# A fused attention and MoE kernel: moe_w_out loaded by column halves, and the second layer's first halves placed among units 5 and 6

## Chip, cores and metric

One Trainium2 chip, one core. The metric is the device time of the kernel in microseconds (us); a profile's own span is some 1.7 us shorter than the time of the same run.

## The reference, cut to what matters

A recurrence over 768 steps (4 batches, 8 heads, head size 48) gives 3072 rows of 384 numbers; two layers follow.

```python
for t in range(S):                      # S = 768
    cur = einsum('bhd,bhe->bhde', u * k[t], v[t])
    y[t] = einsum('bhd,bhde->bhe', r[t], state + cur)
    state = w * state + einsum('bhd,bhe->bhde', k[t], v[t])
x = y.transpose(0, 2, 1, 3).reshape(3072, 384)
h = x @ w_in                            # 384 x 2048
g = h * (1.0 / (1.0 + exp(-h)))
return g @ w_out                        # 2048 x 384
```

## The kernel before

Time is cut into 6 chunks of 128 steps; a **unit** is one chunk of one batch, so there are 24, numbered chunk * 4 + batch. A unit loads r, k and v (`load`), has its rows turned (`p1t`, `p1d`), its scores multiplied and masked (`p2`), its output `y` made (`p3y`, `p3e`), its state brought forward (`sums`, `state`), and its output turned for the two layers (`p4`).

The two layers are **fillers**: a queue of small pieces, taken by `fill(n)` wherever TensorE (PE) would else wait for the recurrence. A first-layer piece for two batches (a "half group": 3 matmuls of 256 columns and one ScalarE activation) has weight 0.5; a second-layer part has weight 1. Both kinds take their PSUM tile from the same three banks (tag `moe`).

```python
    def l1(sc, ft, b0=0, b1=B):                     # first layer
        hps = ps.tile([128, B * C], FP, name="hps", tag="moe", bufs=3)
        ...                                         # 3 matmuls, then ScalarE:
        nc.scalar.activation(out=gts[sc][:, ft, b0 * C:b1 * C], in_=hps, func=AF.Silu)

    def l2(sc, b, part):                            # second layer: 4 parts for each batch
        if part == 0:
            opss[b] = ps.tile([128, HD], FP, name="ops", tag="moe", bufs=3)
        ops = opss[b]
        for ft in range(4 * part, 4 * part + 4):
            nc.tensor.matmul(ops, gts[sc][:, ft, b * C:(b + 1) * C], wout[:, ft, :], ...)
        if part == 3:
            osb = wrk.tile([128, HD], FP, name="osb", bufs=4)
            nc.vector.tensor_copy(out=osb, in_=ops)
            nc.sync.dma_start(out=out[tt:tt + C, :], in_=osb)

    def fill(n):
        owed[0] = min(owed[0] + n, n + 1.0)
        while fillers and owed[0] > 0.01:
            w_, f = fillers.pop(0)
            owed[0] -= w_
            f()
    ...
    def wout_part(g):                               # rows 1024 g to 1024 g + 1023, cast to float16
        nc.gpsimd.dma_start(out=wout[:, 8 * g:8 * g + 8, :], in_=moe_w_out[...])
    ...
    # unit 5 is b_ = B + 1
    p2(b_, nxt=b_ + 1, late=True)                   # with unit 6's turn among unit 5's scores
    fill(1.5)
    p3y(b_)
    p3e(b_)
    p1d(b_ + 1)
    sums(2)
    state(2)
    fill(.5)
    p4(b_)
    fill(1)
    f = l2s(0)
    fillers.extend(l1s(1, 0, 2) + f[0:2] + f[4:6] + f[2:4] + f[6:])
    ...
    for i in range(B + 2, NU):                      # units 6 to 23
        ...
        if i == B + 2:
            half_state(3)                           # float32 state to float16, on ScalarE
        fill(1)
        if sc == 1:
            half_state(b)
        fill(1 if sc in (2, 3) else 2)
```

Of the kernel before, what the change touches and what calls it, by code (L numbers as in the profile page):

```python
# [8 lines left out]
FP = mybir.dt.float32  # L9
# [6 lines left out]
def kernel(  # L16
# [11 lines left out]
    nc = tc.nc  # L28

    B, H, S, D = r.shape  # L30
    C = 128
    NCH = S // C
    HD = H * D
# [4 lines left out]
    NFT = DFF // 128  # L38
# [7 lines left out]
    wrk = ctx.enter_context(tc.tile_pool(name="wrk", bufs=2))  # L46
    ps = ctx.enter_context(tc.tile_pool(name="ps", bufs=1, space=bass.MemoryType.PSUM))
# [11 lines left out]
    wout = big.tile([128, NFT, HD], F16)  # L59

    def unit(i):
        return divmod(i, B)
# [31 lines left out]
    for t in (rin, kin):  # L94
# [7 lines left out]
        out=maskM, in_=maskM, compare_op=ALU.is_ge, fill=0.0,  # L102
# [17 lines left out]
    def spin(n, t=None):  # L120

        if t is None:
            t = ps.tile([128, 512], FP, name="spin", tag="t", bufs=5)
        else:
            t = t.rearrange("s p t -> s (p t)")
        for _ in range(n):
            nc.tensor.matmul(t, junk[:, 0:128], junk, start=True, stop=True)  # L127
# [32 lines left out]
    n = 1  # L160
    while n < C:
        nc.vector.tensor_tensor(
            out=pi[:, :, 1 + n:1 + 2 * n], in0=pi[:, :, 1:1 + n],
# [6 lines left out]
    def lam(g):  # L170

        t = pif.rearrange("q (a n) -> q a n", a=2)[:, :, 0:NT]
        return t.rearrange("q a (p c) -> q a p c", c=C + 1)[:, :, :, 64 * g:64 * g + 64]
# [9 lines left out]
    def nat_ku(i):  # L183
        L = live.setdefault(i, {})
        L["ku"] = wrk.tile([128, H, D], FP, name="ku")
        nc.gpsimd.tensor_tensor(out=L["ku"], in0=kin[i % NIN][:, :, 0:D], in1=u_bc,  # L186
                                op=ALU.mult)

    def nat_rk(i):
        L = live[i]  # L190
        L["rku_f"] = wrk.tile([128, H, D], FP, name="rku_f")
        nc.gpsimd.tensor_tensor(out=L["rku_f"], in0=rin[i % NIN][:, :, 0:D], in1=L["ku"],  # L192
                                op=ALU.mult)

    def nat_kc(i):
        n = i % NIN
        nc.gpsimd.tensor_tensor(out=kc[i % NKC][:, :, 0:D], in0=kin[n][:, :, 0:D],  # L197
                                in1=lamC, op=ALU.mult)
# [37 lines left out]
    def p1t(i):  # L236

        n = i % NIN
        L = live.setdefault(i, {})
        xs = [ps.tile([128, 2, NP, 64], FP, name="xs", tag="t", bufs=5) for _ in range(2)]  # L240
        for a, src in enumerate((rin, kin)):
            flat = src[n].rearrange("p h d -> p (h d)")
            for p in range(NP):
                for g in range(2):
                    t = slice(64 * g, 64 * g + 64)
                    nc.tensor.transpose(xs[g][0:PR, a, p, :],  # L246
                                        flat[t, 128 * p:128 * p + PR], ident[t, t])
        rk = wrk.tile([PR, 2, NP, C], FP, name="rk")
        L["rT"] = rk[:, 0]
        L["kT"] = rk[:, 1]  # L250
        L["xs"] = xs, rk

    def p1d(i):
        L = live[i]
        xs, rk = L["xs"]
        for g in range(2):
            nc.vector.tensor_tensor(out=rk[:, :, :, 64 * g:64 * g + 64], in0=xs[g][0:PR],  # L257
                                    in1=lam(g), op=ALU.mult)
# [6 lines left out]
    def p2(i, spins=0, nxt=None, late=False):  # L265
        L = live[i]
        ae = ps.tile([128, NP, C], FP, name="ae", tag="t", bufs=5)
        ao = ps.tile([128, NP, C], FP, name="ao", tag="t", bufs=5)
        spin(spins, ae)
        for p in range(NP):  # L270
            nc.tensor.matmul(ae[:, p, :], L["kT"][0:D, p, :], L["rT"][0:D, p, :],  # L271
                             start=True, stop=True)
            nc.tensor.matmul(ao[:, p, :], L["kT"][64:PR, p, :], L["rT"][64:PR, p, :],  # L273
                             start=True, stop=True)
        if nxt is not None:
            p1t(nxt)
        L["am"] = []
        for a in (ae, ao):
            am = wrk.tile([128, NP, C], F16, name="am", bufs=4)
            nc.vector.tensor_tensor(out=am, in0=a,  # L280
                                    in1=maskM.unsqueeze(1).broadcast_to([128, NP, C]),
                                    op=ALU.mult)
            L["am"].append(am)
        if nxt is not None and not late:
            p1d(nxt)
# [15 lines left out]
    def p3e(i):  # L301
        L = live[i]
        L["y16"] = wrk.tile([128, H, D], F16, name="y16", bufs=3)
        nc.vector.tensor_tensor(out=L["y16"], in0=L["y"], in1=L["vu"], op=ALU.add)  # L304
# [49 lines left out]
    gts = {}  # L354

    def l1(sc, ft, b0=0, b1=B):
        if sc not in gts:
            gts[sc] = wrk.tile([128, NFT, B * C], F16, name="gT", bufs=2)
        hps = ps.tile([128, B * C], FP, name="hps", tag="moe", bufs=3)
        hps = hps[:, 0:(b1 - b0) * C]  # L360
        for q in range(NQ):
            nc.tensor.matmul(hps, win[:, q, ft * 128:(ft + 1) * 128],  # L362
                             xts[sc][:, q, b0:b1, :].rearrange("p b t -> p (b t)"),
                             start=(q == 0), stop=(q == NQ - 1))
        nc.scalar.activation(out=gts[sc][:, ft, b0 * C:b1 * C], in_=hps, func=AF.Silu)  # L365

    opss = {}

    def l2(sc, b, part):
        if part == 0:  # L370
            opss[b] = ps.tile([128, HD], FP, name="ops", tag="moe", bufs=3)
        ops = opss[b]
        for ft in range(4 * part, 4 * part + 4):
            nc.tensor.matmul(ops, gts[sc][:, ft, b * C:(b + 1) * C], wout[:, ft, :],  # L374
                             start=(ft == 0), stop=(ft == NFT - 1))
        if part == 3:
            osb = wrk.tile([128, HD], FP, name="osb", bufs=4)
            nc.vector.tensor_copy(out=osb, in_=ops)  # L378
            tt = b * S + sc * C
            nc.sync.dma_start(out=out[tt:tt + C, :], in_=osb)  # L380

    def l2_last(sc, b):

        tt = b * S + sc * C
        for n0, n1 in ((0, 256), (256, HD)):
            ops = ps.tile([128, HD], FP, name="ops", tag="moe", bufs=3)
            for ft in range(NFT):
                nc.tensor.matmul(ops[:, n0:n1], gts[sc][:, ft, b * C:(b + 1) * C],  # L388
                                 wout[:, ft, n0:n1],
                                 start=(ft == 0), stop=(ft == NFT - 1))  # L390
            osb = wrk.tile([128, HD], FP, name="osh")
            nc.vector.tensor_copy(out=osb[:, n0:n1], in_=ops[:, n0:n1])
            nc.sync.dma_start(out=out[tt:tt + C, n0:n1], in_=osb[:, n0:n1])

    def l1s(sc, b0=0, b1=B):
        return [((b1 - b0) / B, lambda ft=ft: l1(sc, ft, b0, b1)) for ft in range(NFT)]

    def l2s(sc, b0=0, b1=B):
        return [(1.0, lambda b=b, part=part: l2(sc, b, part))
                for b in range(b0, b1) for part in range(4)]  # L400

    fillers = []
    owed = [0.0]

# [6 lines that stand above are left out]
# [5 lines left out]
    def win_part(c0, c1):  # L416
        nc.gpsimd.dma_start(out=win[:, :, c0:c1],  # L417
                            in_=moe_w_in[:, c0:c1].rearrange("(q p) n -> p q n", p=128))

    def wout_part(g):  # L420
        nc.gpsimd.dma_start(
            out=wout[:, 8 * g:8 * g + 8, :],
            in_=moe_w_out[1024 * g:1024 * g + 1024, :].rearrange("(f p) n -> p f n", p=128))


    p1(0)
# [68 lines left out]
    a, b_ = B, B + 1  # L495
    nat_ku(a)
    nat_rk(a)
    nat_kc(3)
    fill(1)
    p4(3)  # L500
    fill(1000)
# [5 lines left out]
        nat_kc(i)  # L507


    fillers.extend(l1s(0, 2, 4))  # L510
    p1t(a)
    p1d(a)
    bonus_sum(a)
# [10 lines left out]
    p2(a, nxt=b_)  # L524
    nat_ku(b_)
    nat_rk(b_)
    fill(1)
    p3y(a)
    p3e(a)
    wout_part(0)  # L530
    sums(1)
    state(1)
    bonus_sum(b_)
    bonus_vu(b_)
    nat_kc(b_)
    wout_part(1)
    fill(1)
    sums(a)
    state(a)
# [4 lines left out]
    nat_v(b_)  # L544
    for i in range(4):
        load(NIN + i)
    p2(b_, nxt=b_ + 1, late=True)
    fill(1.5)
    p3y(b_)
    p3e(b_)  # L550
    p1d(b_ + 1)
    sums(2)
    state(2)
    fill(.5)
    p4(b_)
    fill(1)
    f = l2s(0)
    fillers.extend(l1s(1, 0, 2) + f[0:2] + f[4:6] + f[2:4] + f[6:])
    sums(b_)
    state(b_)  # L560
    fill(.5)
# [8 lines left out]
    for i in range(B + 2, NU):  # L570
        sc, b = unit(i)
# [27 lines left out]
        if b == B - 1:  # L599
            if sc == 1:  # L600
                f = l1s(1, 2, 4)
# [35 lines left out]
```

## Time and profile before

| | before |
|---|---|
| time, median | 197.33 us (3 runs; 197.08 to 197.41) |
| PE busy, share of the span | 97% |
| matmuls | 1916 |
| unit 5's scores start | 34.45 us |
| unit 6's scores start | 41.17 us |
| unit 13's scores start | 90.04 us |
| unit 23's scores start | 161.49 us, 34.5 us before the end |

The starts of the scores are read from PE's timeline (the first `ae` matmul of a unit). PE is full nearly everywhere, so a shift between two such marks is either idle time or filler put in or taken out.

### The profile page before, as it was taken

Reading aid. Unit: us, or ns where it says so; the run is one execution under the profiler, and the core shown is the slowest. Engines: PE = TensorE matmul, PEld = TensorE weight load, DVE = VectorE, ACT = ScalarE, POOL = GpSimd, SP = SyncE. Lnnn points to the kernel's source line nnn. Section 1 sums busy time; section 2 is a strip of 40 time slices with the busy share of each in tenths; the row PEclk is TensorE's granted clock in tenths of the full one; section 3 lists DMA queues with packets and bytes.
Section 4 is the critical chain, followed back from the end, with each engine's and each line's share of the span. In section 5 each row is a group of like instructions: output and inputs, shape, how many; then the busy total and the mean of one; then the engine's idle time right before and its main releaser. Section 6 shows DMA issues by size and latency. Waiting matters only on the chain.

```text
span 196.0 us, 4920 instructions
## 1 busy us (share of the span) xinstructions
PE 189.3 (97%) x1916; PEld 127.5 (65%) x1916; DVE 115.7 (59%) x233; ACT 91.0 (46%) x207; POOL 115.0 (59%) x145
## 2 busy tenths in 40 slices
PE   7989999899999999999999999999999999999993
PEld 2857788787767887675657656557656556644563
DVE  6787658885767774975486686467576344210121
ACT  3376487799212534216861125692025680069300
POOL 4579969989975779678668737835537710000000
DMA  3999999999697774477356387616461011210022
GB/s 77 222 183 164 154 231 177 186 185 197 132 199 185 161 160 99 108 171 165 75 109 132 106 178 161 131 34 124 114 169 43 20 22 43 92 49 0 3 82 80
DMA packets 89696, 24.12 MB, mean 123 GB/s; under 512 B 82888, under 2 KB 89672, under 8 KB 89672
## 3 DMA queue, kind: packets, MB, share of 16 engines
q1 hardware_dynamic: 85980, 20.65, 48.6%
q0 software_dynamic: 3680, 3.15, 10.7%
q8 instruction: 15, 0.25, 0.6%
q14 instruction: 9, 0.07, 0.1%
q10 hardware_dynamic: 12, 0.00, 0.0%
HBM read 20.45 MB, written 4.72 MB: 128 GB/s over the span
## 4 chain that ended last, share of the span: by engine, by line
PE 82%; POOL 9%; DVE 5%; issue 2%; ACT 0%; POOLq 0%; DVEq 0%
PE ops L374 31%; PE hps L362 27%; PE ae L271 10%; PE xs L246 4%; POOL kc L197 2%; PE spin L127 2%; PE y L297 2%; POOL ku L186 2%; DVE am L280 2%; PE y L294 2%; POOL rku_f L192 2%; POOL vu L209 1%; PE sps L313 1%; PE ops L388 1%; POOL win L417 1%
## 5 line engine op out<-in xcount | busy, mean ns | idle before, releaser
L365 ACT ACTIVATE gT<-hps 128x256 f16<-128x256 f32 (+1 forms) x128 | 59.7, 493 | 51.0 <-PE hps L362 49.3
L362 PE MATMUL hps<-xT,win 128*128 128x256 f16 (+1 forms) x384 | 69.2, 326 | 0.2
L374 PE MATMUL ops<-wout,gT 128*128 128x384 f16 x368 | 63.8, 326 | 0.0
L362 PEld LDWEIGHTS <-win 128*128 128x128 f16 x384 | 35.4, 98 | 23.0 <-issue 0.8
L374 PEld LDWEIGHTS <-gT 128*128 128x128 f16 x368 | 34.7, 98 | 22.4
L280 DVE TENSOR_TENSOR am<-ae,maskM 128x512 f16<-128x512 f32 x24 | 16.6, 691 | 30.5 <-PE ao L273 30.4
L378 DVE COPY osb<-ops 128x384 f32<-128x384 f32 x23 | 12.8, 555 | 28.3 <-PE ops L374 28.1
L271 PEld LDWEIGHTS ae<-rk 48*128 48x128 f32 x192 | 23.1, 187 | 7.7 <-issue 5.1
L271 PE MATMUL ae<-rk 48*128 48x128 f32 x192 | 27.7, 284 | 0.4 <-DVE rk L234 0.4
L209 POOL TENSOR_TENSOR vu<-vin,rku 128x384 f32<-128x384 f32 x23 | 19.1, 829 | 15.1 <-DVE rku L203 15.0
L273 PE MATMUL ao<-rk 48*128 48x128 f32 x192 | 27.7, 285 | 0.0
L186 POOL TENSOR_TENSOR ku<-kin,u_bc 128x384 f32<-128x384 f32 x24 | 24.1, 1006 | 6.0 <-ACT u_bc L153 4.5
L257 DVE TENSOR_TENSOR rk<-xs,pif 112x512 f32<-112x512 f32 x40 | 25.6, 681 | 1.7 <-PE xs L246 1.7
L263 ACT CAST rT<-rk 112x512 f16<-112x512 f32 x20 | 12.3, 615 | 30.2 <-DVE rk L257 30.2
L192 POOL TENSOR_TENSOR rku_f<-rin,ku 128x384 f32<-128x384 f32 x24 | 24.1, 1005 | 1.9
L197 POOL TENSOR_TENSOR kc<-kin,lamC 128x384 f16<-128x384 f32 x24 | 24.0, 1000 | 0.0
L273 PEld LDWEIGHTS ao<-rk 48*128 48x128 f32 x192 | 23.1, 187 | 0.0
L304 DVE TENSOR_TENSOR y<-y,vu 128x384 f16<-128x384 f32 x24 | 13.4, 558 | 9.3 <-POOL vu L209 3.6
L327 POOL CAST stb<-st 112x384 f16<-112x384 f32 x12 | 6.0, 502 | 20.8 <-DVE st L322 20.8
L280 DVE TENSOR_TENSOR am<-ao,maskM 128x512 f16<-128x512 f32 x24 | 16.3, 681 | 0.0
L203 DVE TENSOR_REDUCE rku<-rku_f 128x8 f32<-128x384 f32 x24 | 13.2, 550 | 2.4 <-POOL rku_f L192 2.0
L329 POOL TENSOR_TENSOR sdec<-st,pif 112x384 f32<-112x384 f32 x16 | 13.3, 836 | 0.8 <-ACT gT L365 0.8
(72 smaller groups left out, 169.4 us busy)
## 6 DMA issues: line engine op xcount, KB each, us to landing
rin<-in_r_dram SPq DMA_DIRECT2D x24, 192.0 KB, 3.5
kin<-in_k_dram SPq DMA_DIRECT2D x24, 192.0 KB, 3.4
vin<-in_v_dram SPq DMA_DIRECT2D x24, 192.0 KB, 3.7
out_dram<-osb SPq DMA_DIRECT2D x23, 192.0 KB, 1.9
win<-in_moe_w_in_dram POOLq DMA_DIRECT2D x4, 384.0 KB, 5.8
wout<-in_moe_w_out_dram POOLq DMA_DIRECT2D x2, 768.0 KB, 10.6
xT<-y SPq DMA_TRANSPOSE x18, 2.3
out_dram<-osh SPq DMA_DIRECT2D x1, 128.0 KB, 1.7
```

The costliest lines, as they stand in the source:

```text
L186: nc.gpsimd.tensor_tensor(out=L["ku"], in0=kin[i % NIN][:, :, 0:D], in1=u_bc, op=ALU.mult)
L192: nc.gpsimd.tensor_tensor(out=L["rku_f"], in0=rin[i % NIN][:, :, 0:D], in1=L["ku"], op=ALU.mult)
L197: nc.gpsimd.tensor_tensor(out=kc[i % NKC][:, :, 0:D], in0=kin[n][:, :, 0:D], in1=lamC, op=ALU.mult)
L209: nc.gpsimd.tensor_tensor(out=L["vu"], in0=vin[i % NIN], in1=L["rku"].unsqueeze(2).broadcast_to([128, H, D]), op=ALU.mult)
L257: nc.vector.tensor_tensor(out=rk[:, :, :, 64 * g:64 * g + 64], in0=xs[g][0:PR], in1=lam(g), op=ALU.mult)
L271: nc.tensor.matmul(ae[:, p, :], L["kT"][0:D, p, :], L["rT"][0:D, p, :], start=True, stop=True)
L273: nc.tensor.matmul(ao[:, p, :], L["kT"][64:PR, p, :], L["rT"][64:PR, p, :], start=True, stop=True)
L280: nc.vector.tensor_tensor(out=am, in0=a, in1=maskM.unsqueeze(1).broadcast_to([128, NP, C]), op=ALU.mult)
L304: nc.vector.tensor_tensor(out=L["y16"], in0=L["y"], in1=L["vu"], op=ALU.add)
L362: nc.tensor.matmul(hps, win[:, q, ft * 128:(ft + 1) * 128], xts[sc][:, q, b0:b1, :].rearrange("p b t -> p (b t)"), start=(q == 0), stop=(q ...
L365: nc.scalar.activation(out=gts[sc][:, ft, b0 * C:b1 * C], in_=hps, func=AF.Silu)
L374: nc.tensor.matmul(ops, gts[sc][:, ft, b * C:(b + 1) * C], wout[:, ft, :], start=(ft == 0), stop=(ft == NFT - 1))
```

## The change

The intent: have half of the second layer's work of chunk 0 ready early, as filler that needs only the first half of the columns of moe_w_out, so that PE's holes in unit 5 can be filled and less is left for the end. For this moe_w_out comes in two halves of its columns, the first of them earlier, in the place of unit 3's `kc`, and unit 6's rows are turned in a section of their own behind unit 5's output.

```diff
+    def l2h(sc, b, g, part):                        # half the columns, 2 parts of 8 matmuls
+        if part == 0:
+            opss[b] = ps.tile([128, HD], FP, name="ops", tag="moe", bufs=3)
+        ops = opss[b]
+        n = slice(HC * g, HC * g + HC)
+        for ft in range(8 * part, 8 * part + 8):
+            nc.tensor.matmul(ops[:, n], gts[sc][:, ft, b * C:(b + 1) * C], wout[:, ft, n], ...)
+        if part == 1:
+            ...                                     # copy and store of the half
     def wout_part(g):
-            out=wout[:, 8 * g:8 * g + 8, :],
-            in_=moe_w_out[1024 * g:1024 * g + 1024, :].rearrange("(f p) n -> p f n", p=128))
+        n = slice(HC * g, HC * g + HC)
+        nc.gpsimd.dma_start(out=wout[:, :, n],
+                            in_=moe_w_out[:, n].rearrange("(f p) n -> p f n", p=128))
@@ before unit 4
-    nat_kc(3)
+    wout_part(0)
-    fillers.extend(l1s(0, 2, 4))
+    fillers.extend(l1s(0, 2, 4) + l2hs(0, 0, 0, 2))
@@ unit 4
+    nat_kc(3)
     fill(1)
     p3y(a)
     p3e(a)
-    wout_part(0)
     ...
-    wout_part(1)
@@ unit 5
-    p2(b_, nxt=b_ + 1, late=True)
-    fill(1.5)
+    p2(b_)
+    fill(2)
     p3y(b_)
     p3e(b_)
-    p1d(b_ + 1)
     sums(2)
     state(2)
-    fill(.5)
+    wout_part(1)
+    fill(1)
     p4(b_)
-    fill(1)
-    f = l2s(0)
-    fillers.extend(l1s(1, 0, 2) + f[0:2] + f[4:6] + f[2:4] + f[6:])
+    p1t(b_ + 1)
+    p1d(b_ + 1)
+    fill(1.5)
+    fillers.extend(l1s(1, 0, 2) + l2hs(0, 0, 2, 4) + l2hs(0, 1))
```

More of the change, by code (lines that the diff above doesn't have):

```diff
@@ L370, in l2 @@
         if part == 0:
-            opss[b] = ps.tile([128, HD], FP, name="ops", tag="moe", bufs=3)
-        ops = opss[b]
+            opss[0] = ps.tile([128, HD], FP, name="ops", tag="moe", bufs=3)
+        ops = opss[0]
         for ft in range(4 * part, 4 * part + 4):
@@ L380, in l2 @@
             nc.sync.dma_start(out=out[tt:tt + C, :], in_=osb)
+    def l2h(sc, b, g, part):
[4 more added lines that the diff above has]
+        for ft in range(8 * part, 8 * part + 8):
+            nc.tensor.matmul(ops[:, n], gts[sc][:, ft, b * C:(b + 1) * C], wout[:, ft, n],
+                             start=(ft == 0), stop=(ft == NFT - 1))
+        if part == 1:
+            osb = wrk.tile([128, HD], FP, name="osb", bufs=4)
+            nc.vector.tensor_copy(out=osb[:, n], in_=ops[:, n])
+            tt = b * S + sc * C
+            nc.sync.dma_start(out=out[tt:tt + C, n], in_=osb[:, n])
     def l2_last(sc, b):
@@ L400, in l2s, with l2hs @@
                 for b in range(b0, b1) for part in range(4)]
+    def l2hs(sc, g, b0=0, b1=B):
+        return [(1.0, lambda b=b, part=part: l2h(sc, b, g, part))
+                for b in range(b0, b1) for part in range(2)]
     fillers = []
@@ L418, in win_part @@
                             in_=moe_w_in[:, c0:c1].rearrange("(q p) n -> p q n", p=128))
+    HC = HD // 2
     def wout_part(g):
-        nc.gpsimd.dma_start(
-            out=wout[:, 8 * g:8 * g + 8, :],
-            in_=moe_w_out[1024 * g:1024 * g + 1024, :].rearrange("(f p) n -> p f n", p=128))
+        n = slice(HC * g, HC * g + HC)
+        nc.gpsimd.dma_start(out=wout[:, :, n],
+                            in_=moe_w_out[:, n].rearrange("(f p) n -> p f n", p=128))
     p1(0)
```

## The prediction

> **What bounds the kernel now.** I read the page's busy times first, then the busy time by stretch, then the chain that ended last between 36 and 42 us, then the order of instructions of PE, POOL and the load queue around that place.
>
> The page and the view by stretch (columns: stretch; busy us and count of PE, PEld, DVE, ACT, POOL; granted clock; DMA share; GB/s):
>
> ```profile
> PE 189.3 (97%) x1916; PEld 127.5 (65%) x1916; DVE 115.7 (59%) x233; ACT 91.0 (46%) x207; POOL 115.0 (59%) x145
> ...
> 37.00:39.00 2.00, 1.51 (x26) 1.08 (x24) 1.35 (x3) 0.95 (x3) 1.98 (x4) 1.00 1.19 173
> 39.00:41.17 2.17, 2.10 (x24) 1.64 (x22) 2.09 (x6) 1.81 (x6) 1.41 (x2) 1.00 1.24 176
> 41.17:50.00 8.83, 8.83 (x115) 7.47 (x116) 5.45 (x12) 7.78 (x23) 8.67 (x11) 1.00 1.23 192
> 50.00:60.00 10.00, 10.00 (x117) 6.83 (x113) 7.89 (x15) 2.10 (x5) 8.77 (x10) 1.00 0.79 165
> ...
> 100.00:140.00 40.00, 40.00 (x415) 25.61 (x415) 26.30 (x51) 16.66 (x32) 24.07 (x30) 1.00 0.53 116
> ```
>
> PE is the bound, and from 41.17 us (the weights of unit 6's scores) it has no idle time at all until the tail. So work taken out of PE's queue after 41.17 is worth its full time at the end, and it can only be had by doing it in holes before 41.17. Where the holes are, the chain shows (start us, length us):
>
> ```profile
> 36.14 1.30 DVE am L280 x2
> 37.44 0.05 issue
> 37.48 0.20 PE y L297
> ...
> 38.08 0.57 DVE y L304
> 38.65 0.05 issue
> 38.69 0.36 PE yT L350 x3
> 39.05 0.02 issue
> 39.07 0.49 ACT xT L351
> 39.56 0.04 issue
> 39.60 0.82 PE hps L362 x6
> ```
>
> Unit 5 runs as a relay: VectorE masks, PE multiplies, VectorE adds, PE turns, ScalarE copies, and only then has PE its next matmuls. Taking the matmuls' starts and their spacing (below), PE is idle 0.41 us before y (37.07 to 37.48), 0.38 before yT (38.31 to 38.69), 0.23 before hps (39.37 to 39.60) and some 0.1 at a switch of type: **1.1 us in all, of which 0.7 could be filled**.
>
> **What the Trainium skill says.** (1) "TensorE: Matmul & The Clock Gate", Back-to-back issue gap: a warm matmul of N columns costs N/2.4 + 2.5 ns from start to start. The trace agrees: 12 matmuls of 384 columns took 1.95 us (162.5 ns each), 6 of 256 took 0.656 (109), 12 of 512 took 2.59 (216). The same section's sustained 131 ns for N=512 is not what this trace has. (2) "DMA: Bandwidth & Descriptors", Specifications: 512 B is the smallest transfer for line rate. In this trace packets of 192 B go at 12 GB/s an engine and ones of 1536 B at 20 to 23. (3) Same page, SWDGE vs HWDGE vs iDMA: a casting DMA has to be issued from GpSimd, which builds the descriptors; and under Queues, rings and completion order, an engine takes turns between queues packet by packet. The trace agrees on the turns: between 43 and 47 us both queues moved about 192 packets in each us.
>
> **The change, part by part.**
> *Column halves.* 64 matmuls of 384 columns become 128 of 192. By the two measured sizes, (162.5 - 109.3)/128 = 0.416 ns a column, so 82.7 ns for 192 columns; two cost 165.4 against 162.5. Weight loads don't bind: the turned 128-column blocks, each with its own load, go at 57 ns. 64 x 2.9 ns = **+0.19 us** of PE. The copies and stores become 8 of half the size instead of 4, on VectorE and DMA with room: nothing on the path.
> *Earlier fillers.* Fill sections up to the scores of unit 6 take, before, 20 half groups of the first layer (3 matmuls of 109 ns, 0.327 us each): 6.54 us. After, by counting weights and what is owed, 16 half groups and 4 half parts of 8 x 82.7 ns = 0.66 us: 5.23 + 2.65 = 7.88 us. So 1.33 us of filler moves ahead of unit 6, and the scores of unit 6 start later by what doesn't fit a hole. From 38.31 on: l2 part 0.66, yT 0.17, the turn of unit 6 0.45 (gone from between the scores and the filler of unit 5), three more l2 parts 1.98, two sums 0.34, switches 0.15: 42.06 instead of 41.17, +0.89 us. The hole before y grows by 0.1, since VectorE, busy without a break from 31.17 to 37.43, still delivers at 37.43. **Net -0.44 us.** With the 0.19 back: **-0.25 us**, if nothing new waits.
> *moe_w_out earlier, in the place of unit 3's kc.* On POOL it starts when rku_f of unit 4 ends (start us, length us):
>
> ```profile
> 28.07 1.00 POOL L192 TENSOR_TENSOR rku_f<-rin,ku 128x384 f32<-128x384 f32 x1
> 29.03 0.99 POOL L197 TENSOR_TENSOR kc<-kin,lamC 128x384 f16<-128x384 f32 x1
> ...
> 34.55 0.94 POOL L421 DMA_DIRECT2D wout<-in_moe_w_out_dram  x1
> ...
> 38.04 0.94 POOL L421 DMA_DIRECT2D wout<-in_moe_w_out_dram  x1
> ```
>
> so 5.5 us earlier, at 29.0; kc moves to the first transfer's old place and is needed only after 41. But the first l2 part is now wanted at 38.3 instead of 47.5. Before, the first transfer landed 9.7 us after its issue. Reading the queues us by us: first packets at 37.2 (2.7 after issue), 1024 packets until 42.7 (5.5 us), landing 1.5 later. Now each half is 2048 rows of 768 B. The time of a packet: in the middle of the transfer
>
> ```profile
> q0 software_dynamic: 195, 0.15, 104.2%
> q1 hardware_dynamic: 58, 0.01, 9.2%
> ```
>
> (packets, MB, share, for the us from 38 to 39) 195 in 1 us on 16 engines is 82 ns each; the loads' 192 B take 15.4 ns, stores of 512 B 28 ns and of 1536 B 68 ns, which lie on 8 ns + 0.039 ns/B. That gives 38 ns for 768 B; the casting queue was 1.2 times over that line at 1536 B, so I choose 45: 128 x 45 ns = 5.8 us. Landing at 29.0 + 2.7 + 5.8 + 1.5 = **39.0**, a wait of **0.7 us** before the first l2 part. A wait there moves everything behind it one for one, as PE is full from there.
> *wout's second half* goes out near 40 and is wanted past 52: hidden. *Unit 6's turn* after unit 5's yT costs no more than in the old place, and frees two score banks in between.
> Sum: 197.33 - 0.44 + 0.19 + 0.7 = **197.8 us**.
>
> **The rivals.**
> *A, no wait: the gain as designed.* If wout's packets flow at 38 ns and start as they did, it lands at 38.1 and the time is 197.33 - 0.25 = 197.1. For it: the linear rule for packets, and that the parts are laid out as if tuned to this. It can't be much more: holes of 0.7 us are all there is, so over 2% (3.95 us) faster is out of reach.
> *B, the packet count rules.* w_in's packets of 2048 B went at 188 to 200 a us, hardly slower than the 195 of wout's 1536 B. If a casting packet has a fixed cost near 75 ns, 2048 of them take 9.6 us, landing is at 42.8, the wait 4.5 us and the time 201.6. Against it: the stores' and loads' packets scale with bytes, and w_in is close to an engine's full rate (2048 B in 84 ns is 24 GB/s), so its speed doesn't tell of a fixed cost.
> *C, starved loads.* While wout flowed at 38 to 40 us the loads got nearly nothing (one took 14.4 us to land). Moved to 32 to 38, this hits the loads of units 6 to 8. Unit 6's rows are nearly in by 32; unit 7's are wanted at 43. With 4 us between the halves at 1000 packets a us they catch up; at worst 1 to 2 us: 198.5 to 199.5.
> *D, a later queue run dry.* Queued filler is lower by 2 weights for the rest of the run; at the end of chunk 2 that is 0 instead of 2, so the first-layer groups of chunk 2 come right after unit 11's turned block lands (issued at 83.10, landing 2.3 later, first use after the change near 84.9 in the same clock). Its store ahead in the queue also comes earlier, so about 0 to 0.5 us.
>
> **Range and chances.** A has perhaps 0.35, a wait of 0.3 to 2 us 0.35, 2 to 4 us 0.2, more 0.1. That puts the middle at 197.8 and 8 of 10 between 196.8 and 200.4. Slower by over 2% (above 201.3) needs B in full or B with C: 0.06. Faster by over 2% (under 193.4): 0.01. Within 2%: 0.93.
>
> **What would show it.** In the changed profile: matmuls of 128x192 at 82 to 84 ns from start to start; wout issued on POOL near 29.0, with its landing 9.5 to 10.5 us later (under 9.3: A; over 12: B); the idle time of PE just before the first ops matmul, near 38.3, with the wout DMA as releaser and 0.7 us long; no more holes at yT and hps of unit 5; the scores of unit 6 at 42.1 plus the wait; PE full from there. Wrong would be: VectorE's masks of unit 5 moving (a change ahead of 37 us that I took as fixed), idle PE behind unit 6 (C or D), or POOL held for over 1.5 us by the longer descriptor list.

## More of the kernel before

One more view is needed later: PE and ScalarE (ACT) after unit 6's scores, from the timeline of the kernel before (start us, length us, engine, line, operation, tiles, shape, count; in brackets the idle time before it and its releaser).

```profile
42.71 2.30 PE L362 MATMUL hps<-xT,win 128*128 128x256 f16 x18
...
45.48 2.13 PE L362 MATMUL hps<-xT,win 128*128 128x256 f16 x18
47.45 1.46 PE L374 MATMUL ops<-wout,gT 128*128 128x384 f16 x8
```

```profile
47.28 0.61 ACT L263 CAST rT<-rk 112x512 f16<-112x512 f32 x1
47.78 0.51 ACT L334 CAST stb<-st 112x384 f16<-112x384 f32 x1
48.20 0.66 ACT L365 ACTIVATE gT<-hps 128x256 f16<-128x256 f32 x2
```

PE does 12 half groups (two runs of 18 matmuls), then second-layer parts from 47.45. Just then ScalarE leaves the first layer for two casts (47.28 to 48.20), and PE doesn't notice, since its second-layer parts wait for nothing from ScalarE.

## The result, and the profile after

The time was **200.32 us** (median of 6 runs, 199.71 to 201.22) against 197.39 for the kernel before in the same rounds (6 runs, 197.08 to 198.05). The ratio is 1.015, 95% interval 1.012 to 1.018: slower, by less than 2%. Ratios here and below are the mean time of one kernel's fast runs over that of the other's of the same rounds, so not quite the ratio of the medians that are quoted.

The profiled run was the fastest of the six. By the starts of the scores, its span is longer than that of the kernel before by 2.0 us as follows.

| stretch | before, us | after, us | difference |
|---|---|---|---|
| start to unit 5's scores | 34.45 | 34.14 | -0.31 (differs from run to run, -0.8 to +0.3) |
| unit 5's to unit 6's | 6.72 | 7.82 | +1.10 |
| unit 6's to unit 13's | 48.87 | 51.07 | +2.20 |
| unit 13's to unit 23's | 71.45 | 71.46 | 0 |
| unit 23's to the end | 34.5 | 33.5 | -1.0 |

Everything is decided between 34 and 93 us; the last line is the filler that has been done earlier (eight matmuls of 384 columns, 1.30 us), less 0.26 us by which the span runs on longer behind VectorE's last copy (2.92 us, before 2.66; all profiles with the column halves show it, and its cause was not looked for). The page and the stretches after (same columns as the prediction's):

```profile
PE 189.9 (96%) x1980; PEld 131.7 (67%) x1980; DVE 116.3 (59%) x237; ACT 90.8 (46%) x207; POOL 115.6 (58%) x145
```

```profile
37.00:39.00 2.00, 1.84 (x32) 1.67 (x32) 1.32 (x4) 0.77 (x2) 1.75 (x3) 1.00 1.10 221
...
45.00:50.00 5.00, 4.12 (x46) 3.38 (x45) 2.79 (x7) 4.45 (x15) 4.92 (x6) 1.00 1.38 184
50.00:60.00 10.00, 9.85 (x152) 9.28 (x151) 5.99 (x14) 3.38 (x9) 6.21 (x8) 1.00 0.77 165
60.00:70.00 10.00, 9.75 (x132) 8.40 (x131) 7.11 (x15) 4.19 (x11) 8.29 (x10) 1.00 0.78 171
```

The holes of unit 5 are mostly filled: PE is busy 1.84 us of the stretch from 37 to 39, not 1.51. The hole before y, though, has grown: from 0.43 us to 0.58 in two pieces (0.73 in the second profile, after_again), 0.26 of it a half group that waits for ScalarE. But behind unit 6's scores, where PE was full before, it is busy only 4.12 of the 5 us from 45, and short of full again until 70, and once more at 88. PE's timeline says for what:

```profile
45.88 0.34 PE L313 MATMUL sps<-v,kc 128*128 128x96 f16 x4 [0.19 <-POOL kc L197]
46.06 2.46 PE L362 MATMUL hps<-xT,win 128*128 128x256 f16 x21
49.21 1.45 PE L362 MATMUL hps<-xT,win 128*128 128x256 f16 x9 [0.69 <-ACT gT L365]
...
64.21 1.18 PE L362 MATMUL hps<-xT,win 128*128 128x256 f16 x9 [0.25 <-DVE osb L393]
...
87.86 2.10 PE L362 MATMUL hps<-xT,win 128*128 128x512 f16 x9 [0.17 <-DMA xT<-y]
```

The brackets count from the modelled end of a matmul, which overlaps the next one. From one start to the next, at the measured spacing, the holes are larger: 0.36 before the sums at 45.88, 0.85 before 49.21, 0.40 within the nine matmuls after it (1.45 us where 9 x 109 ns are 0.98), 0.41 before 64.21 and 0.34 before 87.86. That is **2.36 us**, and it covers the +2.20 of the table. The kernel before has none of them. The first, for kc, comes with the new order as well: five half groups stand between unit 6's scores and its y where there were six, so that PE comes to the sums 0.57 us sooner after the scores, and POOL has kc ready only 0.2 us sooner. The largest two, 1.25 us, end with a ScalarE activation:

```profile
44.04 1.04 ACT L365 ACTIVATE gT<-hps 128x256 f16<-128x256 f32 x3 [1.60 <-PE hps L362]
...
46.59 1.37 ACT L365 ACTIVATE gT<-hps 128x256 f16<-128x256 f32 x4 [0.55 <-PE hps L362]
47.85 0.61 ACT L263 CAST rT<-rk 112x512 f16<-112x512 f32 x1
48.36 0.51 ACT L334 CAST stb<-st 112x384 f16<-112x384 f32 x1
48.77 0.66 ACT L365 ACTIVATE gT<-hps 128x256 f16<-128x256 f32 x2
49.31 0.52 ACT L334 CAST stb<-st 112x384 f16<-112x384 f32 x1
```

ScalarE does the same casts at the same place as before. What is new is what PE has to do beside them. Its four second-layer parts have been spent ahead of unit 6's scores, so only first-layer half groups are left: 15 between the scores of units 6 and 7, where there were 12 and then two second-layer parts. ScalarE had no activation to do from 42.4 to 44.04 (1.60 us idle), while PE worked on second-layer parts and scores; then it gets the bunch together with the casts. From 47.85 on a cast of rT and one of stb hold the activations up by 0.9 us. PE runs on for the three banks, 0.98 us at 0.327 us each, and then stands until the first activation behind the casts ends (48.77 + 0.38 = 49.15; PE starts at 49.21).

The wait that the prediction had its eye on is not there in this profile: the first second-layer part starts at 38.02 with no idle time before it. A line of POOL's timeline and one of the page's DMA issues (count, KB each, median us from issue to landing) belong to it:

```profile
28.62 1.20 POOL L443 DMA_DIRECT2D wout<-in_moe_w_out_dram  x1
```

```profile
wout<-in_moe_w_out_dram POOLq DMA_DIRECT2D x2, 768.0 KB, 10.3
```

The first half was issued 5.9 us earlier than before and landed 9.1 us later, just in time.

### The profile page after: what moved, and what is told of

Read it like the earlier page. It is cut to its first block, busy times and chain, and to the rows that moved or that the text cites. A ratio compares the mean times of both kernels' runs of the same rounds, so it can differ in the third digit from the quotient of the medians.

```text
span 198.0 us, 5058 instructions
## 1 busy us (share of the span) xinstructions
PE 189.9 (96%) x1980; PEld 131.7 (67%) x1980; DVE 116.3 (59%) x237; ACT 90.8 (46%) x207; POOL 115.6 (58%) x145
## 3 DMA queue, kind: packets, MB, share of 16 engines
q0 software_dynamic: 5728, 3.15, 12.4%
## 4 chain that ended last, share of the span: by engine, by line
PE 77%; POOL 10%; DVE 5%; issue 3%; DMA 2%; ACT 2%; POOLq 0%; DVEq 0%
PE hps L362 25%; PE ops L374 24%; PE ae L271 9%; PE ops L389 5%; PE xs L246 4%; POOL kc L197 2%; PE spin L127 2%; POOL rku_f L192 2%; DVE am L280 2%; POOL ku L186 2%; DMA xT<-y 2%; PE y L297 2%; PE y L294 2%; PE sps L313 1%; PE ops L403 1%
## 5 line engine op out<-in xcount | busy, mean ns | idle before, releaser
L374 PE MATMUL ops<-wout,gT 128*128 128x384 f16 x304 | 52.9, 326 | 0.0
L374 PEld LDWEIGHTS <-gT 128*128 128x128 f16 x304 | 28.7, 98 | 18.4
L378 DVE COPY osb<-ops 128x384 f32<-128x384 f32 x19 | 10.6, 558 | 32.2 <-PE ops L374 32.0
## 6 DMA issues: line engine op xcount, KB each, us to landing
wout<-in_moe_w_out_dram POOLq DMA_DIRECT2D x2, 768.0 KB, 10.3
```

## The experiments

Two theories stood. **Transfer:** the early moe_w_out is late at its first use, or starves the loads. **Order:** the second-layer parts were taken from a place where they covered for ScalarE. The table shows each run's profile against that of the kernel before in the same stretches (us), and the timed ratio. The runs fell into three calls, each on its own chip; runs of different calls are compared only through their ratios to the kernel before.

| run | to 5 | 5 to 6 | 6 to 13 | 23 to end | span | ratio (95%) |
|---|---|---|---|---|---|---|
| after | -0.31 | +1.10 | +2.20 | -1.0 | +2.0 | 1.015 (1.012-1.018) |
| after_again | +0.02 | +2.20 | +2.01 | -1.0 | +3.2 | 1.017 (1.013-1.021) |
| e_halves | -0.64 | 0.00 | +1.16 | +0.3 | +0.8 | 1.005 (1.002-1.008) |
| e_turn | +0.05 | +0.45 | +0.39 | -0.6 | +0.3 | 1.000 (0.996-1.003) |
| e_early | +0.05 | +2.43 | +1.07 | 0.0 | +3.5 | 1.015 (1.012-1.019) |
| e_early_turn | +0.23 | +0.47 | +1.82 | -0.6 | +1.9 | 1.009 (1.005-1.014) |
| e_order | +0.24 | +1.82 | +2.20 | -1.0 | +3.3 | 1.016 (1.011-1.020) |
| e_keep67 | +0.32 | +1.73 | -0.01 | +0.3 | +2.3 | 1.015 (1.010-1.020) |
| e_both | -0.76 | +3.72 | 0.00 | +0.3 | +3.2 | 1.017 (1.012-1.022) |
| e_late | -0.02 | +1.47 | -0.57 | +0.3 | +1.1 | 1.007 (1.003-1.010) |
| e_vec | -0.30 | +2.16 | -0.61 | +0.3 | +1.5 | 1.011 (1.006-1.016) |
| e_all | +0.06 | +1.90 | -0.97 | +0.3 | +1.2 | 1.004 (1.001-1.007) |

Between units 13 and 23 every run of the table agrees within 0.02 us. e_noload, whose start was spoilt, is not in the table.

### after_again: the changed kernel once more

No edit; a second profile.

> The changed kernel once more, for a second profile and more times. In its first profile TensorE's new idle stretches after 40 us are 0.85 and 0.40 us at first-layer matmuls waiting for ScalarE (48 to 51 us), 0.41 us for a score bank (63.8), 0.34 us for unit 11's turned block (87.5) and 0.36 us for kc of unit 6 (45.5). All theories: 199.7 to 201.2 us again. Theory ORDER (the sixteen first-layer groups of units 4 and 5 now come bunched behind the scores of unit 6, and ScalarE can't keep up): the waits at 48 to 51 us are here again and about as long, 1.0 to 1.6 us. Theory DRY (two weights less in the queue, so chunk 2's first layer starts when unit 11's block has just landed): the wait near 87 us is longer in a run that is slower. Theory LOAD (moe_w_out earlier starves the loads, or lands after its first use): idle time at 30 to 43 us that grows in a slower run.

Measured: 200.90 us against 197.75. Here the wait is there:

```profile
38.18 0.49 PE L362 MATMUL hps<-xT,win 128*128 128x256 f16 x3
39.44 0.75 PE L389 MATMUL ops<-wout,gT 128*128 128x192 f16 x7 [0.77 <-DMA wout<-in_moe_w_out_dram]
```

From start to start it is 1.26 - 0.33 = 0.93 us: issue at 29.10, landing 10.3 us later. Behind unit 6, the holes for kc (0.38), ScalarE (0.86, and again the shorter one within the nine matmuls) and the bank (0.41) are the same as in the first profile; the one for xT near 88 us is not there. So the first profile was a lucky one as to the transfer, and the later holes but the last are no accident.

### e_halves: the column halves alone

The kernel before, with `l2h`, `l2hs` and the column form of `wout_part` at the old places:

```diff
-    f = l2s(0)
-    fillers.extend(l1s(1, 0, 2) + f[0:2] + f[4:6] + f[2:4] + f[6:])
+    fillers.extend(l1s(1, 0, 2) + l2hs(0, 0) + l2hs(0, 1))
```

> The kernel before, with the column halves alone: both loads at the places they had, chunk 0's second layer in column halves after all first-layer groups of units 4 and 5, nothing moved into units 5 and 6. By the matmul arithmetic of the prediction it costs 64 times 2.9 ns, 0.19 us: 197.3 to 197.9. If the smaller packets or stores, or score banks at the seam to chunk 1, are what costs, over 198.2.

Measured: 198.69 us against 197.75, +0.9 us. The matmuls of 192 columns run at 83 ns, as worked out, which makes 0.19 us. In the profile the end is 0.25 us longer too (the longer run-out behind the last copy, see above). The rest is one stall from 55 to 58 us that nobody had thought of, on VectorE:

```profile
57.97 0.36 DVE L393 COPY osb<-ops 128x192 f32<-128x192 f32 x1 [3.10 <-DMA out_dram<-osb]
```

Twice as many copies take twice as many of the four `osb` buffers, and here VectorE waits 3.10 us for a store to give one back. PE's y of unit 8 then waits 0.84 us in two pieces for the masks behind it. The changed kernel doesn't show this hole in its trace; it belongs to the halves in the old order.

### e_turn: unit 6's turn moved, alone

```diff
-    p2(b_, nxt=b_ + 1, late=True)
-    fill(1.5)
+    p2(b_)
+    fill(2)
     p3y(b_)
     p3e(b_)
-    p1d(b_ + 1)
     ...
     p4(b_)
+    p1t(b_ + 1)
+    p1d(b_ + 1)
```

> The kernel before, with unit 6's turn alone moved to behind unit 5's turn of y (and a fill of 2 in place of 1.5 before unit 5's y, as in the change). It puts 0.45 us of turns into the holes of 0.38 and 0.23 us around 39 us, so by the prediction 0.2 to 0.4 us faster than before: 197.0 to 197.3. If the place of the turn is what costs (VectorE gets unit 6's blocks later), slower than 197.6.

Measured: 197.76 us against 197.75, no difference. The hole of 0.23 before hps is filled, that of 0.38 before yT stays, and the one before y grows from 0.43 to 0.55, as the half group put in (0.33 us) is shorter than the turn taken out (0.45). The hoped-for gain of a few tenths did not come.

### e_early: the early transfer alone

The kernel before, its first half by rows, issued in the place of `kc`:

```diff
     nat_rk(a)
-    nat_kc(3)
+    wout_part(0)
     fill(1)
     ...
     nat_rk(b_)
+    nat_kc(3)
     fill(1)
     p3y(a)
     p3e(a)
-    wout_part(0)
```

> The kernel before, with only the first row half of moe_w_out moved to where the change puts it (in place of kc of unit 3, which goes behind unit 5's rku_f). LOAD: if the early transfer is what costs, this is slower than before by 0.5 us or more, with TensorE waiting for loads between 30 and 45 us. ORDER and DRY: the order of the matmuls is as before, so within 0.3 us of before (197.4).

Measured: 201.00 us against 197.75, as slow as the whole change, without a single half part. Nothing waits for moe_w_out here. PE's waits name something else (us in total, times, longest):

```profile
PE xs L246 <- DMA kin<-in_k_dram: 2.7, 1, 2.7
...
PE hps L362 <- ACT gT L365: 0.9, 1, 0.9
```

Unit 6's k now takes 9.5 us to land, where it took 3.7: its packets stand behind those of moe_w_out. In the changed kernel this load is just as late (9.0 us), and there it costs nothing. The next run says why.

### e_early_turn: early transfer and moved turn

The edits of e_early and e_turn together.

> The kernel before, with the first row half of moe_w_out early AND unit 6's turn behind unit 5's turn of y. With the early half alone TensorE stood 2.7 us at unit 6's turn for kin of unit 6 (landing 9 us after issue, while moe_w_out flowed). LOAD-1: the early half costs through that one wait, and the later turn is there to step around it; then this is within 0.5 us of before: 197.3 to 198.3. LOAD-2: the starved loads cost again further on (unit 7's rows, vin of 6), so this stays over 198.8.

Measured: 199.62 us (five runs) against 197.36, ratio 1.009. The wait of 2.7 us for k is gone. So **the turn's own section is what makes the early transfer bearable**: it puts the first use of unit 6's rows some 3.7 us later. What is left is the next late load, in ScalarE's and PE's timelines:

```profile
47.02 0.51 ACT L181 CAST v<-vin 128x384 f16<-128x384 f32 x1 [1.54 <-DMA vin<-in_v_dram]
```

```profile
47.87 1.36 PE L362 MATMUL hps<-xT,win 128*128 128x256 f16 x11 [1.27 <-ACT gT L365]
```

ScalarE stands 1.54 us for unit 7's v, activations queue up behind the cast, and PE waits 1.44 us from start to start. Read by PE's releaser alone this would be "ScalarE too slow"; only ScalarE's own line shows the load.

### e_order, e_keep67 and e_both: give ScalarE back its cover

e_order mixes second-layer parts into the bunch:

```diff
-    fillers.extend(l1s(1, 0, 2) + l2hs(0, 0, 2, 4) + l2hs(0, 1))
+    f, g = l1s(1, 0, 2), l2hs(0, 0, 2, 4)
+    fillers.extend(f[:5] + g[:2] + f[5:10] + g[2:] + f[10:] + l2hs(0, 1))
```

e_keep67 takes less filler in units 6 and 7, so that the queue is as long afterwards as in the kernel before:

```diff
-        fill(1 if sc in (2, 3) else 2)
+        fill(1 if sc in (1, 2, 3) else 2)
```

e_both has the two edits.

> The changed kernel, with the same fillers in another order behind unit 5: the four half parts of the second layer for batches 2 and 3 are put between the first-layer groups of units 4 and 5 instead of behind all sixteen. ORDER: the waits for ScalarE at 48 to 51 us (0.85 and 0.40 us in the first profile of the changed kernel, 0.86 in the second) go, and the time falls by 0.8 to 1.2 us against the changed kernel, to 199.3 to 200.0. LOAD: those waits are not what costs; no more than 0.3 us.

> The changed kernel, with the last fill of units 6 and 7 at 1 in place of 2, so that from unit 8 on the queue holds as many fillers as before. DRY: the waits for a score bank near 64 us (0.41 us in both profiles) and for unit 11's turned block near 87 us (0.34 in one profile) go, 0.4 to 0.8 us faster than the changed kernel: 199.7 to 200.3. Otherwise no gain.

> The changed kernel with both edits, the order and the kept fillers. ORDER and DRY together: 1.2 to 2.0 us faster than the changed kernel, 198.6 to 199.4, and what is left over before (1.2 to 2 us) is LOAD: the wait for moe_w_out at its first use and unit 5's holes. If this is no better than the changed kernel, the waits it takes away only made room for others.

Measured against 197.36: 201.02, 200.53 (five runs) and 200.94 us, by the ratios none better than the change. In e_order the wait for ScalarE is gone, and another stands at the same place:

```profile
47.35 1.48 PE L389 MATMUL ops<-wout,gT 128*128 128x192 f16 x16
...
50.38 1.14 PE L362 MATMUL hps<-xT,win 128*128 128x256 f16 x9 [0.89 <-DVE osb L393]
```

A finished second-layer tile keeps its bank until VectorE has copied it, and VectorE gets to it only at 49.96, behind a `y` add that had itself waited 1.36 us for POOL. With three banks for both layers, taking one for `ops` at this place is no better than waiting for ScalarE: 1.05 us against 0.85 + 0.40. My theory of the order, as far as it said that mixing would cure it, fell.

In e_keep67 the wait for a bank at 64 us is gone from the profile, and with it the shorter of the two for ScalarE, so these two did come from what units 6 and 7 take from the queue. The wait for xT at 88 us is absent too, but so it is in after_again, e_order and e_noload, which have the shorter queue: it comes and goes. The filler left out, 1.3 us, is done at the end instead (+0.3 in place of -1.0 in the table), which costs nothing in the sum; beyond that the two stretches of the table are together 0.7 to 0.9 us shorter than in the two profiles of the change. The times don't show this (ratio 1.015, as the change has). Why is not shown; the wait for moe_w_out ahead of it differs by more than that from profile to profile.

In e_both moe_w_out took 11.8 us to land, the longest of all, and the first half part waited 2.41 us for it.

### e_noload: no first transfer (wrong)

The first half of `wout` is set to a constant by VectorE at the start, and POOL does a multiplication in the transfer's place.

```diff
+    nc.vector.memset(wout[:, :, 0:HD // 2], 0.02)
+    busy = cst.tile([128, H, D], FP)
...
-    wout_part(0)
+    nc.gpsimd.tensor_tensor(out=busy, in0=u_bc, in1=u_bc, op=ALU.mult)
```

> Wrong on purpose: the changed kernel without the early load of moe_w_out's first column half. The half is set to 0.02 by VectorE in the first microseconds, and a GpSimd multiply of about 1 us stands where GpSimd issued the load; everything else is the change. LOAD-WAIT: what the early half costs is TensorE's wait for it at its first use (0, 0.93, 0.65, 0.60 and 2.41 us in the five profiles with that order) and the loads it holds up; without it 0.9 to 1.6 us faster than the changed kernel: 199.1 to 199.9. The rest (ScalarE's bunch of groups, kc of unit 6, banks at 64 us, 1.6 to 2.2 us) stays. If the load is not a cost, as fast as the changed kernel (200.3 to 200.9); if it is the whole cost, 197.1.

Measured: 203.85 us (four runs) against 197.71, and useless as a time. The memset took 2.62 us at 3.5 us, ahead of VectorE's decay table; PE stood 5.6 us and lost its clock (by stretch; the granted clock is the third number from the right):

```profile
10.00:15.00 5.00, 0.96 (x8) 0.99 (x10) 4.83 (x6) 1.68 (x5) 1.84 (x2) 0.74 1.03 169
15.00:20.00 5.00, 5.00 (x48) 4.15 (x45) 3.69 (x8) 2.10 (x9) 0.35 (x1) 0.58 0.46 92
```

That PE falls to half its clock after an idle window of some 3.4 us is in the Trainium skill, "TensorE: Matmul & The Clock Gate", Part 1; this trace agrees: PE stands from 8.4 to 14.0 us, and the clock granted from 12.4 to 19.2 us is 0.50 (hence 0.74 and 0.58 as means of the two stretches). From 19.3 to 99.2 us it is 1.00, so two local readings can be kept, though the run as a whole was slow. The first: no wait for moe_w_out at the first half part, and 7.80 us from unit 5's scores to unit 6's, next to 7.82 in the lucky profile of the change and 8.92 in the other. The second is about what comes behind unit 6:

```profile
52.25 0.34 PE L315 MATMUL sps<-v,kc 128*128 128x96 f16 x4 [0.19 <-POOL kc L199]
52.43 2.46 PE L364 MATMUL hps<-xT,win 128*128 128x256 f16 x21
55.58 1.45 PE L364 MATMUL hps<-xT,win 128*128 128x256 f16 x9 [0.69 <-ACT gT L367]
```

Without the first transfer the waits for kc and for ScalarE stand there as in the changed kernel, and so does the one for a bank (0.42); the stretch from unit 6's scores to unit 13's is 50.86 us, +1.99. So these waits do not come from the early transfer. This is what decides between the two theories in that stretch. A cleaner version, with the constant set at a time when VectorE is free, was not run.

### e_late: use the first half a little later

e_keep67, with half a weight of filler moved behind unit 6's turn:

```diff
     wout_part(1)
-    fill(1)
+    fill(.5)
     p4(b_)
     p1t(b_ + 1)
     p1d(b_ + 1)
-    fill(1.5)
+    fill(2)
```

> e_keep67 (the changed kernel with the last fill of units 6 and 7 at 1) with the first half part of the second layer moved behind unit 5's turn of y and unit 6's turn, some 1 us later. LOAD-WAIT: the wait at first use falls from 0.6 to 2.4 us to 0 to 1.4, a hole of 0.38 us before unit 5's yT comes back; in all 0.3 to 0.7 us faster than e_keep67 (200.8): 200.1 to 200.5. Otherwise no gain.

Measured: 198.96 us against 197.71, ratio 1.007 where e_keep67 had 1.015: some 1.6 us better, though on another chip.

```profile
38.68 0.34 PE L350 MATMUL yT<-ident,y 128*128 128x128 f16 x3 [0.22 <-DVE y L304]
...
39.54 1.49 PE L389 MATMUL ops<-wout,gT 128*128 128x192 f16 x16
```

The hole at yT is back (0.39 from start to start), and the first half part starts 0.86 us later and doesn't wait (landing at 38.7). In the profiles this makes 0.26 us between the scores of units 5 and 6; 0.57 more lies behind unit 6, where the waits for kc (0.36) and for unit 8's k (0.18, in e_keep67 alone) are gone. The wait for ScalarE stays at 0.86. So the very hole that the change was made to fill could be given up at no loss; how much of the 1.6 us is the wait for moe_w_out, this run doesn't tell.

### e_vec: the state's casts on VectorE

e_keep67, with the `half_state` copies of units 6 and 7 done by VectorE:

```diff
-            half_state(3)
+            half_state(3, nc.vector.tensor_copy)
...
-            half_state(b)
+            half_state(b, nc.vector.tensor_copy)
```

> e_keep67 with the casts of the state for units 6 and 7's batches (two of them stand between ScalarE's first-layer groups at 48 to 50 us, 0.52 us each) on VectorE. ORDER, second test, since e_order only turned the wait for ScalarE into one for a score bank: the waits of 0.85 and 0.40 us near 50 us fall by 0.8 us or more, and the time by 0.6 to 1.0: 199.8 to 200.2. If another wait takes their place as in e_order, no gain.

Measured: 199.78 us (four runs) against 197.71, ratio 1.011 (1.006 to 1.016).

```profile
49.88 0.49 PE L362 MATMUL hps<-xT,win 128*128 128x256 f16 x3 [0.28 <-ACT gT L365]
```

The wait for ScalarE goes from 0.85 to 0.44 us, as two casts of 0.5 us leave ScalarE there; the wait for moe_w_out was 0.99 in this profile. Since nothing else was touched, this is the plainest evidence that the casts on ScalarE, beside a bunch of half groups, are what PE waits for. It is evidence from the trace: the times of e_vec and e_keep67 (1.010 to 1.020) don't tell the two apart.

### e_all: both

> e_keep67 with both edits of e_late and e_vec: if the waits are separate costs, 0.9 to 1.7 us faster than e_keep67: 199.1 to 199.9, still slower than before (197.4), since unit 5's holes are only 0.6 us and the halves cost 0.2.

Measured: 198.59 us against 197.71, ratio 1.004 (1.001 to 1.007). Left are a hole of 0.39 at yT, 0.32 for moe_w_out (0.46 with the switch of type before it) and 0.45 for ScalarE. It has the lowest time of all forms of the change, though e_late's interval overlaps with it, and it is still 0.8 us behind the kernel before. No version beat that.

## Why the prediction was right or wrong

It said 197.8 us, 196.8 to 200.4, and within 2% with 0.93. The time was 200.32, within 2% and at the upper edge of the range. The mechanism of its own wait was right; its sum of +0.45 us was short by 2.5. That the range held the result is in part luck: its upper end was there for a longer wait for moe_w_out and for starved loads, and most of the 2.5 us was neither. The prediction did name "idle PE behind unit 6" as a sign of being wrong, but with C or D as the cause.

- **PE as the bound, gain limited to 0.7 us of holes: right.** The yT and hps holes of unit 5 are filled (the one before y grew by 0.15 to 0.3, where 0.1 was predicted), unit 6's scores come at 41.96 (42.1 predicted without the wait), and between units 13 and 23 nothing changes.
- **Column halves, 83 ns each: right.** What e_halves cost beyond 0.19 us was mostly a wait for a store buffer: the prediction saw VectorE and DMA "with room" there, and there was none.
- **Transfer: right in kind, and near in the sum because errors cancelled.** In the six profiles with this order it was issued at 28.4 to 29.3 (29.0 predicted) and landed 10.3 us later in the mean (10.0). But the first packet came 1.9 to 2.2 us after the issue (2.7), the packets flowed for 6.8 to 8.4 us (5.8), and landing was 0.3 to 0.4 us behind the last packet in five of the six (1.5, read in the kernel before, where the second half was issued 3.5 us behind the first). From 33 to 34 us, one of its densest:

```profile
q0 software_dynamic: 438, 0.17, 146.4%
```

  438 packets in 1 us on 16 engines are 36.5 ns each (34 in the densest us, with 471), under the line's 38 and not the 45 chosen; later they shared the engines with loads (291 and 290 packets in one us of after_again), and the flow took longer than predicted. The wait at the first use was 0, 0.93, 0.65, 0.60, 2.41 and 0.99 us in the six profiles with this order, 0.93 in the mean, for a predicted 0.7. (The 0.60 is e_keep67's; the profile puts it down to ScalarE, but moe_w_out landed at 39.22 and PE started at 39.27, the distance seen in e_order too.) Rival B, a fixed cost for each packet, is out.
- **Rival C, starved loads: half right.** The loads moved as few as 0 to 86 packets a us while moe_w_out flowed, and k of unit 6, which the prediction had "nearly in by 32", landed at 37.95, 9.0 us after issue. Alone this costs 2.7 us (e_early). I had taken the turn's move as a matter of holes and banks; it is what dodges this.
- **Rival D, the short queue: seen once.** 0.34 us at 87.86, in the range of 0 to 0.5, but in one of the four profiles with the short queue (not in after_again, e_order or e_noload). The wait for a bank (0.41) was not foreseen; it left with e_keep67.
- **Net -0.44 "if nothing new waits": the step that failed.** It treated fillers as time alone, so that 1.33 us of them could be moved and PE would be "full from there". But a second-layer part needs nothing from ScalarE, and a half group needs an activation and a bank. Moving four second-layer parts ahead took the cover from ScalarE's casts behind unit 6; PE stood there for 1.25 us. In the terms of the sum: the stretch from unit 6 to unit 13 was to grow by 0.19 (the halves) and grew by 2.0 to 2.2: 1.25 for ScalarE, 0.36 for kc, 0.41 for a bank and, in the first profile, 0.34 for xT, less some switches of type that my count of holes includes. The end was to shrink by 1.33; the filler there did, by 1.30, but the run-out behind the last copy grew by 0.26. The stretch from unit 5 to unit 6 was to grow by 1.7 with the wait (0.89 and 0.1 and 0.7) and grew by 2.1 in the mean of the six profiles.

So the expected gain went first into the wait for moe_w_out, and more than all of it was lost once more behind unit 6, most to ScalarE, which had been off the critical path because of the order of the fillers. Shown in the traces by taking away: in the changed kernel the early transfer is not what makes PE wait behind unit 6 (e_noload); two of ScalarE's casts are worth 0.41 of the 0.85 us there (e_vec); the wait for a bank and the shorter one for ScalarE leave with e_keep67. The times confirm of all this only that e_late and e_all are faster than the change. **What stays open:** how much the first wait is in runs without a profile, as it went from 0 to 2.4 us between profiles; what a clean run without the transfer would take, as e_noload spoilt its own start; what part of e_late's gain is the first wait; and the 0.26 us behind the last copy.

## What to carry to other kernels

Filler work has a kind as well as a length: before moving pieces in a queue, write down for each piece which other engine and which buffers it needs, and see whether the stretch it leaves still feeds all of them at the rate that they can take. An early transfer is to be priced by the loads that it delays and not only by its own landing; and where its landing varies by microseconds, a hole of a few tenths just before it can be cheaper than work that waits for it (e_late). When PE waits for ScalarE, look at what ScalarE itself was waiting for or doing.

## What the Trainium skill lacked or had wrong

- "DMA: Bandwidth & Descriptors", Queues, rings and completion order: turns between queues packet by packet. (Its packet is a group of descriptors; the trace counts rows of 192 and 384 B.) That held late in a transfer (after_again, 36 to 37 us: 291 packets of the casting queue and 290 of loads), but not early in one: in the changed kernel the loads had 86, 11, 0 and 34 packets in the four us from 31 to 35, beside 173, 471, 438 and 468 of moe_w_out, with unit 6's k issued and not landed; whether its packets stood ready in their queue, the trace doesn't show. The page gives no figure for what a GpSimd-issued transfer does to the landing of other loads (k of unit 6: from 3.7 to 9.0 us).
- The same page, Specifications: 512 B as the least size for line rate; it does not say whether of the bytes read or written. Rows of 768 B read and 384 B written went at 36.5 ns, 21 GB/s an engine by bytes read, no slower than the rows of 1536 B read and 768 B written of the kernel before (19 to 21). The page has no time of a packet by size for casting transfers.
- "TensorE: Matmul & The Clock Gate", Back-to-back issue gap: the sustained spacing of 131 ns for 512 columns and 81 for 128. Measured were 216 and 56; its isolated formula fits both, and the 83 ns for 192 columns.
- "ScalarE: Activation LUTs", What ACT_TABLE_LOAD costs: 186 ns + 0.833 ns a column, less 93 back to back, so 306 ns for 256 columns in a row (an estimate from it). One activation took 384 ns and two in a row 0.66 us, 0.28 from start to start, a little less than that and under PE's 0.327.
